# RWKV-7 attention and a SwiGLU feed-forward: the first chunk without its state terms, and a new order of all steps

## The chip, the cores and the metric

The kernel runs on one core of a Trainium2 chip. Such a core has TensorE (PE) for matrix products, with PEld for its weight loads, VectorE (DVE), ScalarE (ACT), GpSimd (POOL) and SyncE (SP); SP, ACT and POOL issue DMAs, and each engine works through its own instructions in order. The engines wait for each other by semaphores. The metric is the device time of one execution in microseconds, the median of several; lower is better.

## The reference

Two blocks follow each other: a recurrent attention over 768 steps for 4 x 8 heads of width 40, and a feed-forward layer on its output (3072 tokens of width 320, inner width 1536).

```python
state = np.zeros((B, H, D, D), dtype=np.float32)
for t in range(S):
    kt, vt, rt = (k[:, :, t], v[:, :, t], r[:, :, t])
    wt, at, bt = (w[:, :, t], a[:, :, t], b[:, :, t])
    y[:, :, t] = np.einsum('bhd,bhde->bhe', rt, state)
    Sa = np.einsum('bhde,bhe->bhd', state, at)
    state_decay = state * wt[:, :, None, :] - np.einsum('bhd,bhe->bhde', Sa, bt)
    state = state_decay + np.einsum('bhd,bhe->bhde', vt, kt)
...
rms = np.sqrt(np.mean(x * x, axis=-1, keepdims=True) + 1e-06)
xn = x / rms * rms_g
g = xn @ w_gate
silu = g * (1.0 / (1.0 + np.exp(-g)))
val = xn @ w_val
return (silu * val @ w_out).astype(np.float32)
```

The state is zero at the start. The weights of the feed-forward layer come as 64-bit numbers, and the kernel turns them into 32-bit ones itself.

## The kernel before

The 768 steps are cut into 24 chunks of 32. Within a chunk the recurrence becomes products and a triangular solve; only the state goes from chunk to chunk. The work of a chunk c has these stages:

- `front(c)`: loads k, v, w, a, b of the chunk (tiles `wan`, `kbn`, `wn`, `VU`), turns them on TensorE, and builds by five levels of doubling (groups `gramk`) the triangular matrix `LT`, the scaled keys `KN` and the decays `T`. At its end `LT` goes out to DRAM and comes back turned as `M`.
- `inverse(c)`: the triangular solve on VectorE: 31 rounds of two small operations (`tmp<-Yi,M` and `Yi<-Yi,tmp`), in sequence. Its result goes out and back into `LT` by DMA.
- `main(c)`: with the state `ST` and its turned copy `Sd`. A group `state` and a first group `lower` make the right side X; a second group `lower` multiplies it by the inverse; `update` gives the new state, to which VectorE adds the old one, decayed (`Sdec`). Then the output, with r loaded for two chunks at a time: `score`, masks (`As`), five `level` groups and a `y0` group (the part that comes from the state), decays and additions of `y` on VectorE, two turns, the norm.
- `feed(g)`: for every two chunks the feed-forward layer on 256 tokens, in twelve slices of the inner width taken in pairs: groups `h64` and `h` (gate and value), the silu on ScalarE (`sg`), a product on VectorE (`hT`), and `out`, which sums over the slices in PSUM (`po`).
- `narrow(f, h, ...)`: once per half slice, the change of weights from 64 to 32 bits: loads into a buffer `wf`, eight steps on VectorE and ScalarE (those on VectorE with one input are TENSOR_SCALARs of 128x480, such as `ex<-wf`; one of three buffers for `ex` is the tile `o`), and a store into `sW` in DRAM.

None of this code issues an instruction when it runs. Each call of `pe`, `tt`, `copy`, `dma`, `blank` and so on makes a `Piece` (L258), and `plan.issue(ORDER, PAIRS)` (L993) issues the pieces in an order that stands in the file as a list of numbers, `ORDER` (L45): each number is the place of the next piece among those not issued yet, and "-" is a filler, a product of the identity with itself into an unused part of `po` (L991). `PAIRS` (L247) says for each use of PSUM which of three double banks (`ps0` to `ps2`) it gets. What matters of the order is each engine's own sequence, and with it what a queue holds up.

The zeros that pad the tiles are set by GpSimd at the start: `blank` is a MEMSET, and `Turns` (L587) calls it for the tiles that ask for it (`wan`, `kbn`, `rn`, `wn`, `VU`, `ST`, `LT`, `Sd`, `A`, `y`; each recorded at L514). They are pieces like all others and have their place in the order. GpSimd also issues most loads of `front` after the first chunk (recorded at L518). All VectorE operations of helpers are recorded at L475, copies of ScalarE at L502, activations at L498, groups of products at L521, turns at L524.

Of the kernel before, what the change touches and what calls it, by code (L numbers as in the profile page):

```python
# [16 lines left out]
P = 128  # L17
# [28 lines left out]
27 33 37 36 26 32 42 38 39 348 40 41 1 110 31 43 0 26 1 14 27 263 - 17 194 2 28 0 41 342 - 16 18 0 41 14 42 43 - 55  # L46
60 72 175 47 84 48 58 186 44 45 8 185 589 54 59 - 70 - - 68 93 69 601 176 49 - 53 - 590 179 16 57 71 80 180 603 50 -
81 92 67 65 624 56 613 51 626 - 66 - 614 52 - 188 64 187 627 178 - 637 - 177 0 8 - - 188 - 60 82 61 78 76 - 81 77
637 75 - 62 388 90 599 624 601 72 194 87 88 74 89 384 73 590 101 196 195 395 84 85 94 197 591 96 86 394 209 385 399
93 592 102 201 202 213 212 225 223 0 94 213 - 10 592 225 223 - 388 - 237 - 233 197 - 395 - - 246 - - 593 - 613 594 -  # L50
- - 221 614 595 234 385 596 615 649 397 - 198 202 - 648 616 617 647 - 207 386 - - 4 328 597 206 602 618 603 210 646
- 220 619 203 218 96 0 603 203 329 16 - 204 208 213 97 0 0 242 33 216 6 34 23 2 0 173 589 590 604 81 201 325 591 199
380 220 219 11 83 163 164 214 313 592 216 326 174 228 200 210 610 213 655 0 299 626 300 359 187 583 584 199 565 287
615 1069 577 197 629 198 211 585 586 362 183 566 587 1068 616 0 78 125 135 302 0 0 87 299 151 302 0 0 0 0 0 300 72
301 311 81 322 837 324 0 0 0 246 844 126 0 126 294 0 0 296 132 302 840 0 0 129 131 0 827 304 0 - 242 130 315 297 327
296 241 0 0 0 0 295 0 295 305 0 296 307 0 316 0 0 543 - 298 0 0 0 0 0 297 310 0 278 0 278 0 - 278 0 290 - - 317 - -
0 0 289 0 283 301 58 261 0 0 - 0 0 301 280 291 246 296 109 281 300 0 0 307 254 105 245 292 0 103 292 305 304 0 0 0
102 286 297 0 0 298 285 312 0 0 - 0 0 0 0 291 0 0 248 0 287 0 293 0 296 801 94 0 0 788 93 789 471 300 0 93 483 94 95
797 96 292 471 472 0 289 483 464 96 97 472 98 99 290 484 100 101 465 466 102 473 515 103 104 105 474 295 294 485 106
107 0 295 292 474 107 108 475 485 476 486 109 110 111 515 492 493 112 487 494 488 113 114 115 116 1 3 0 493 115 0  # L60
378 379 371 0 179 406 0 406 385 0 0 0 - 375 0 382 383 375 0 - - 414 - - - 413 - 383 - - - - - - - - 0 - - - - - - -
- - - - - - - - - - - - - - - - - - - - - - - - - - - - - 0 - - - - - - - - - - 410 - - 409 382 383 - - 0 0 0 370 33
- 35 37 - 36 0 0 0 - 0 0 29 - - - - - 0 40 32 0 0 0 38 - 372 373 411 41 30 39 81 410 - 0 91 231 42 43 51 81 41 373
46 - 48 45 39 229 49 44 90 - 0 46 57 58 0 398 - 52 399 385 386 228 0 0 0 397 634 50 384 637 0 0 0 48 246 0 51 394
150 0 401 631 0 1 2 0 637 398 390 391 376 146 43 377 626 399 638 392 218 378 636 147 635 393 400 430 47 431 148 48
149 49 - 150 50 - 151 401 402 152 242 153 154 - 51 379 243 0 379 642 644 842 - 832 154 155 643 419 833 645 51 380
657 52 646 156 662 674 157 158 - 647 686 649 53 54 402 650 651 843 - 159 656 655 660 55 160 - 161 671 - 56 57 673 -
652 706 162 1 658 163 659 669 2 164 3 0 - 610 608 107 335 603 108 612 609 - 614 109 - - 595 - 110 624 - 625 - 111
636 - - 596 - - - - - - 605 - 112 - 590 345 382 373 - - 782 346 383 607 384 626 622 792 620 113 114 - 115 627 - -
374 375 385 783 - 606 116 635 - 617 - - - 793 - 117 623 376 118 - 619 377 119 378 621 120 618 160 634 121 - 379 122  # L70
- 633 - 380 - - 161 123 124 386 125 381 163 - 164 387 - 388 162 - - 126 127 - 128 629 - - - 389 390 - 631 - 391 129
130 131 630 - 167 639 - 132 133 134 135 640 168 638 - 392 393 430 - 641 136 - 137 138 394 - 165 581 - 431 139 140
141 166 644 - - 142 171 571 721 143 570 580 643 144 145 - 173 - 645 - 175 146 147 148 - 174 172 182 178 - 179 149 -
- 177 637 180 642 150 - 176 189 185 186 432 187 191 732 190 778 788 787 0 282 283 37 18 584 1064 626 1065 284 625
583 41 628 582 568 635 19 498 42 43 285 44 643 286 0 480 637 44 568 598 498 499 500 644 286 501 502 570 45 287 288
503 908 898 643 600 645 494 504 601 657 505 662 506 3 897 649 674 0 649 45 705 46 906 47 - 494 1 506 660 669 659 672
670 48 0 622 633 598 636 645 - 632 458 - 459 0 - 595 0 595 458 853 642 0 360 755 - 765 361 - 505 - 764 362 363 364
500 504 508 507 365 501 502 516 518 503 0 0 45 0 514 43 363 364 365 512 366 367 41 417 419 421 368 369 2 - 3 - - -
370 371 372 418 0 - 372 0 416 426 0 - 369 504 37 426 370 371 372 373 374 375 376 377 378 379 380 381 526 429 525 521
520 505 382 0 482 466 9 396 390 - 377 391 393 392 400 398 343 430 378 387 397 - - 440 344 429 439 580 394 395 408  # L80
345 403 388 11 700 0 0 0 401 402 700 403 343 344 473 345 406 0 406 0 705 708 402 697 474 406 407 707 487 0 0 5 406 0
406 470 485 693 703 8 407 469 480 37 483 0 0 335 41 402 30 480 336 337 338 0 0 400 0 40 39 400 335 336 337 472 0 337
703 705 400 401 699 907 37 338 470 481 402 478 27 704 339 340 479 899 700 341 701 343 486 714 403 28 889 50 719 0
861 673 451 684 677 530 531 313 869 458 11 0 682 867 878 19 554 0 0 9 699 683 684 10 0 10 710 11 12 0 0 38 39 11 551
527 12 0 23 37 659 669 36 704 - 436 670 681 679 539 296 682 680 692 691 703 24 660 677 3 678 676 4 675 435 0 656 657
658 667 432 0 0 40 0 426 19 290 20 685 42 707 292 291 679 21 665 681 41 22 433 40 53 666 30 680 686 23 0 288 681 30
0 30 432 433 434 692 22 674 690 0 0 8 653 0 8 9 667 651 662 0 16 25 17 37 9 0 26 8 400 654 0 652 8 651 38 400 - 39 -
- 37 - - 667 659 - - 469 9 - - - 401 402 403 10 668 16 17 661 0 0 392 650 24 460 461 458 0 36 458 461 8 37 392 647
14 393 15 394 16 395 49 50 47 5 396 397 17 18 19 462 463 729 0 3 583 21 22 458 14 15 392 572 4 461 646 0 0 388 568
640 18 389 11 19 577 390 0 622 0 6 370 371 618 0 435 28 440 0 14 431 438 5 436 370 6 26 432 693 694 7 440 8 0 0 432  # L90
362 0 7 427 686 441 425 0 361 0 440 6 7 430 0 0 352 7 732 353 0 0 0 351 352 13 0 727 8 442 422 352 423 737 353 735
738 726 354 355 356 736 357 419 0 354 355 356 5 730 357 721 358 359 360 361 362 363 364 365 6 0 419 420 742 365 366
367 368 369 423 370 371 372 373 424 0 0 674 423 424 425 6 0 737 732 746 368 369 370 0 429 419 420 735 992 993 1003
1150 668 1002 670 1151 669 685 730 439 368 584 732 421 731 0 0 3 367 368 369 583 370 983 420 584 585 734 586 587 371
735 742 686 421 422 423 424 685 745 756 740 743 992 758 747 744 982 746 757 755 759 768 767 0 3 424 735 0 0 0 0 581
582 772 745 747 583 744 421 730 584 365 746 731 732 431 0 3 440 584 585 586 740 2 425 587 588 1 589 590 741 591 783
365 742 752 366 761 762 757 592 756 368 367 0 5 172 173 174 175 176 337 6 0 333 346 332 176 0 346 176 330 8 9 0 224
176 177 178 179 180 181 9 12 182 183 184 185 186 187 188 561 225 189 190 226 10 227 0 224 0 226 180 181 6 0 0 13 0
214 223 325 178 179 180 181 182 183 184 185 186 187 13 188 189 190 215 224 191 192 193 276 267 0 263 274 414 20 323
222 223 191 192 193 194 334 324 0 4 331 194 330 332 195 226 229 230 225 0 222 223 226 227 240 239 532 232 4 0 229 4  # L100
0 7 12 233 234 333 193 317 326 321 324 533 334 235 239 540 331 332 531 532 236 543 13 14 240 335 241 195 242 243 244
612 8 196 245 541 542 336 548 0 193 5 190 242 0 328 329 330 0 541 330 331 236 543 539 332 237 238 737 239 240 6 745
538 540 544 552 545 735 397 557 569 581 556 16 746 555 542 728 566 551 546 736 241 565 398 727 550 553 563 568 738
# [290 lines left out]
def kernel(  # L394
# [34 lines left out]
    B, H, S, D = r.shape  # L429
# [5 lines left out]
    NCH = S // C  # L435
# [364 lines left out]
    def main(c):  # L800
# [21 lines left out]
        if c + 1 < NCH:  # L822
            tt(ST_.next()[:, :, :, 0:D].rearrange("p n i d -> p i n d"),
               up[:, :, 0:N * D].rearrange("p i (n d) -> p i n d", n=N),
               Sdec.rearrange("p (n i) d -> p i n d", n=N), ADD)
# [198 lines left out]
```

## Time and profile before

Three runs took 1142.61, 1139.24 and 1142.14 us, the median being 1142.14. The profiled execution took 1138.7 us, with a span of 1136.9 us from its first to its last instruction.

| engine | busy us | share of the span | instructions |
|---|---|---|---|
| PE | 1042.0 | 92% | 23166 |
| PEld | 858.4 | 76% | 23166 |
| DVE | 912.9 | 80% | 3069 |
| ACT | 447.8 | 39% | 988 |
| POOL | 303.5 | 27% | 533 |

Of the PE's busy time 66.3 us are the fillers (446 records, two for each). The costliest groups are those of the feed-forward layer, 358.1 us for gate and value and 182.1 us for the last product, and on VectorE the two operations of the solve, 157.9 and 155.9 us. The chain of work that ended last lies on PE for 56% of the span, on DVE for 29%, and 6% of it is time in which an engine waited for nothing that the profile shows ("issue").

The page cuts the span into 40 equal slices and gives each engine's busy share in tenths, and for PE the granted clock, in tenths of full speed. Other views give sums for a stretch of time, the operations of one tile with their durations (least, median, most), or the instructions in order of time. [...]

### The profile page before, as it was taken

What the parts mean: (1) busy time and instruction counts of PE and PEld (TensorE: products, weight loads), DVE (VectorE), ACT (ScalarE), POOL (GpSimd) and SP (SyncE); (2) the same over time, 40 slices, a digit from 0 to 9 for tenths busy, and PEclk for the clock granted to TensorE, in tenths of its full rate; (3) what the DMA queues carried; (4) which work ended last, traced back from release to release, by engine and by line L of the source; (5) the groups of instructions that cost most, each with busy time, mean ns of one, the idle gap of its engine ahead of it and who ended that gap; (6) DMA issues with size and microseconds to landing.
All of it is one profiled execution on the core that took longest, in us unless ns stands there. A gap on an engine that the chain in (4) does not pass through costs nothing.

```text
span 1136.9 us, 53105 instructions
## 1 busy us (share of the span) xinstructions
PE 1042.0 (92%) x23166; PEld 858.4 (76%) x23166; DVE 912.9 (80%) x3069; ACT 447.8 (39%) x988; POOL 303.5 (27%) x533
## 2 busy tenths in 40 slices
PE   5678889889999999999999999999989999999998
PEld 4667778667778777778877877777768787777876
DVE  5899999799787998799699699889878799697421
ACT  4543544653253343344333434334335335323211
POOL 6530333113223223223223313332313423100000
PEclk9769899899999999999999999999999999999999
DMA  7445442776555546446545545545546545444242
GB/s 152 98 106 170 119 119 63 206 224 159 136 138 123 120 102 153 128 109 153 134 117 134 126 116 141 133 116 142 116 100 158 122 111 141 102 112 124 77 151 64
DMA packets 171177, 145.43 MB, mean 128 GB/s; under 512 B 123712, under 2 KB 142080, under 8 KB 170944
## 3 DMA queue, kind: packets, MB, share of 16 engines
q1 hardware_dynamic: 152576, 119.06, 38.9%
q0 software_dynamic: 16192, 22.64, 10.3%
q8 instruction: 182, 2.98, 1.1%
q10 hardware_dynamic: 2176, 0.33, 0.2%
q14 instruction: 51, 0.42, 0.1%
HBM read 125.83 MB, written 16.12 MB: 125 GB/s over the span
## 4 chain that ended last, share of the span: by engine, by line
PE 56%; DVE 29%; issue 6%; DMA 3%; ACT 3%; POOL 2%; SPq 1%; DVEq 0%; ACTq 0%; POOLq 0%
PE ps L521 37%; PE po L521 10%; PE ps L524 7%; DVE Yi L475 5%; DVE tmp L475 5%; DVE LT L475 3%; DVE K L475 3%; DVE y L475 2%; DVE hT L475 1%; DVE Ab L475 1%; POOL kbn L518 1%; DVE ex L475 1%; DVE As L475 1%; PE po L991 1%; DMA wan<-in_w_dram 1%
## 5 line engine op out<-in xcount | busy, mean ns | idle before, releaser
L521 PE MATMUL ps<-xg,wf 128*128 128x256 f32 (+1 forms) x1728 | 358.1, 395 | 7.0 <-DVE hT L475 1.7
L521 PEld LDWEIGHTS ps<-xg,wf 128*128 128x128 f32 (+1 forms) x1728 | 264.7, 191 | 64.1 <-issue 18.4
L521 PE MATMUL po<-wf,hT 128*128 128x320 f32 x576 | 182.1, 448 | 2.9 <-DVE hT L475 2.9
L475 DVE TENSOR_TENSOR tmp<-Yi,M 128x60 f32<-128x60 f32 (+24 forms) x744 | 157.9, 212 | 18.4 <-DMA M<-sB 1.0
L475 DVE TENSOR_TENSOR Yi<-Yi,tmp 128x60 f32<-128x60 f32 (+24 forms) x744 | 155.9, 210 | 17.4
L498 ACT ACTIVATE sg<-ps 128x256 f32<-128x256 f32 x144 | 54.0, 384 | 242.0 <-PE ps L521 231.6
L518 POOL DMA_DIRECT2D VU<-in_v_dram x92 | 53.2, 585 | 351.7 <-PE ps L521 193.7
L521 PEld LDWEIGHTS po<-wf,hT 128*128 128x128 f32 x576 | 103.0, 191 | 38.1 <-DVE hT L475 5.0
L475 DVE TENSOR_TENSOR hT<-ps,sg 128x256 f32<-128x256 f32 x144 | 59.8, 421 | 64.7 <-ACT sg L498 63.5
L521 PEld LDWEIGHTS ps<-Ab,K 40*64 40x64 f32 x4608 | 78.2, 138 | 33.5 <-issue 19.3
L521 PE MATMUL ps<-Ab,K 40*64 40x56 f32 x4608 | 87.8, 225 | 15.7 <-DVE Yi L475 5.7
L502 ACT COPY KN<-ps 128x640 f32<-128x640 f32 x96 | 66.4, 691 | 79.5 <-PE ps L521 37.5
L475 DVE TENSOR_TENSOR K<-K,T 128x512 f32<-128x512 f32 (+1 forms) x192 | 92.6, 490 | 4.5 <-PE ps L521 2.6
L475 DVE TENSOR_TENSOR As<-ps,msi 128x256 f32<-128x256 f32 (+1 forms) x192 | 82.8, 483 | 10.8 <-PE ps L521 10.8
L502 ACT COPY K<-K 128x256 f32<-128x256 f32 (+1 forms) x168 | 71.7, 443 | 46.2 <-DVE K L475 24.1
L521 PEld LDWEIGHTS ps<-As,KN 128*40 128x40 f32 x3072 | 65.4, 123 | 17.9 <-issue 10.8
L518 POOL DMA_DIRECT2D kbn<-in_b_dram x92 | 53.9, 588 | 93.5 <-PE ps L521 91.9
L518 POOL DMA_DIRECT2D wn<-in_w_dram x92 | 51.9, 570 | 99.6 <-DVE tmp L475 47.7
L521 PE MATMUL ps<-As,KN 128*40 128x32 f32 x3072 | 72.8, 204 | 4.0 <-issue 2.6
L518 POOL DMA_DIRECT2D kbn<-in_k_dram x92 | 53.5, 585 | 71.5 <-PE ps L521 62.3
L991 PE MATMUL po<-ident 128*128 128x128 f32 x446 | 66.3, 302 | 5.3 <-ACT po L544 5.3
L475 DVE TENSOR_TENSOR y<-y,ps 128x256 f32<-128x256 f32 x120 | 50.4, 420 | 23.2 <-PE ps L521 18.5
(123 smaller groups left out, 1571.7 us busy)
## 6 DMA issues: line engine op xcount, KB each, us to landing
wf<-sW SPq DMA_DIRECT2D x144, 480.0 KB, 4.1
M<-sB SPq DMA_DIRECT2D x96, 128.0 KB, 3.8
rn<-in_r_dram SPq DMA_DIRECT2D x24, 160.0 KB, 4.4
sW<-ex SPq DMA_DIRECT2D x16, 240.0 KB, 3.7
out_dram<-o SPq DMA_DIRECT2D x48, 80.0 KB, 3.7
kbn<-in_b_dram POOLq DMA_DIRECT2D x92, 40.0 KB, 3.3
wan<-in_w_dram POOLq DMA_DIRECT2D x46, 80.0 KB, 3.8
wan<-in_a_dram POOLq DMA_DIRECT2D x46, 80.0 KB, 4.0
```

The costliest lines, as they stand in the source:

```text
L475: plan.add("DVE", time + more + each * size(o), 0.087, lambda at: fn(at(o), *m(at)), [o], aps(*args))
L498: scalar(o, [a], lambda at: nc.scalar.activation(at(o), at(a), f, **kw), aps(acc), 0.1 if f in (AF.Square, AF.Relu) else 0.0)
L502: scalar(o, [a], lambda at: nc.scalar.copy(at(o), at(a)), extra=more)
L518: plan.add(by, 0.6 if by == "POOL" else 0.45, 0.0, lambda at: queue.dma_start(out=o, in_=i), [o], [i], load=LOADS[load], since=since)
L521: return o, lhsT, rhs, lambda at: nc.tensor.matmul(at(o), lhsT, rhs, start=start, stop=stop, skip_group_check=True), 4
L524: return o, i, ident, lambda at: nc.tensor.transpose(at(o), i, ident), 2
L991: plan.warm = lambda: nc.tensor.matmul(po_[:, 0, DM:DM + P], ident, ident, start=False, stop=False, skip_group_check=True)
```

## The change

Two things change. First, chunk 0 drops the terms of the state, which is zero there: the `state` group, the decay `Sdec`, the addition of the decayed state (the new state is a copy by ScalarE instead), the `y0` group with its copy and its decay, and the addition of level 16, for which half of `y` is set to zero by GpSimd and the other half copied by ScalarE. Second, `ORDER` and `PAIRS` are new from end to end.

```diff
-        pe("state", [mm(X[other(i, n), o, col(n % 4)], ...
-        pe("lower", [mm(X[other(i, n), o, col(n % 4)], LT[own(i, n), o * N + slot(n)], VU[own(i, n), n, o, 0:D], False, n % 4 == 3)
+        if c > 0:
+            pe("state", [mm(X[other(i, n), o, col(n % 4)], ...
+        pe("lower", [mm(X[other(i, n), o, col(n % 4)], LT[own(i, n), o * N + slot(n)], VU[own(i, n), n, o, 0:D], c == 0 and n % 4 == 0, n % 4 == 3)
...
-        tt(Sdec, ST.rearrange("p n i d -> p (n i) d")[:, :, 0:D], z["T"][32].to_broadcast((P, NI, D)), MUL)
+        if c > 0:
+            tt(Sdec, ST.rearrange("p n i d -> p (n i) d")[:, :, 0:D], z["T"][32].to_broadcast((P, NI, D)), MUL)
...
-        if c + 1 < NCH:
+        if c == 0:
+            copy(ST_.next()[:, :, :, 0:D].rearrange("p n i d -> p i n d"), up[:, :, 0:N * D].rearrange("p i (n d) -> p i n d", n=N))
+        elif c + 1 < NCH:
...
-        pe("y0", [mm(y0[part(o), i, n], ...
+        if c > 0:
+            pe("y0", [mm(y0[part(o), i, n], ...
...
-        copy(yi[:, :, :, 0:16], y0[:, :, :, 0:16])
-        tt(yi[:, :, :, 16:], y0[:, :, :, 16:],
-           z["T"][16].rearrange("p (n i) x -> p i n x", i=2)[:, :, :, 0:1].to_broadcast((P, 2, N, 16)), MUL)
-        down(4, yl[:, 0])
+        if c > 0:
+            copy(yi[:, :, :, 0:16], y0[:, :, :, 0:16])
+            tt(yi[:, :, :, 16:], y0[:, :, :, 16:],
+               z["T"][16].rearrange("p (n i) x -> p i n x", i=2)[:, :, :, 0:1].to_broadcast((P, 2, N, 16)), MUL)
+            down(4, yl[:, 0])
+        else:
+            blank(y[:, :, 0:16], 0.0)
+            copy(y[:, :, 16:], yl[:, 0].rearrange("p n (i l) -> p (n i) l", i=2))
```

`ORDER` has 6131 pieces and 223 fillers before, 6127 pieces and 280 fillers after. What the new order does to GpSimd's first instructions, from the two programs' lists (a load is one DMA issue):

```
before  ... load kbn2 | ST0 rn0 y1 wn0 VU0 Sd0 ST1 VU1 | load VU1, load kbn2, 3 loads VU1 | y0 | loads
after   ... load wan | ST0 | load kbn2 | kbn2 y1 | 3 loads kbn2 | rn0 y0 | load kbn2 | wn0 VU0 | load VU1 |
            Sd0 ST1 | load VU1, load kbn2 | y0 (half) | 2 loads VU1 | VU1 | loads
```

The names without "load" are MEMSETs of these tiles; the half `y0` is the new one.

## The prediction

> **What bounds the kernel now.** I read the busy share over time first, then the sums of single stretches, then the timeline of the places these pointed to. In the page's second part the digits are busy tenths in slices of 28.4 us:
>
> ```profile
> PE   5678889889999999999999999999989999999998
> DVE  5899999799787998799699699889878799697421
> PEclk9769899899999999999999999999999999999999
> ```
>
> The kernel has two parts. In the first eight slices (to about 230 us) VectorE is at 8 to 9 and TensorE below it; from the ninth on TensorE is at 9. The sums by stretch say it sharper (columns: stretch, its length, busy us and count of PE, PEld, DVE, ACT, POOL, granted clock, DMA share, GB/s):
>
> ```profile
> 35.00:41.00 6.00, 0.00 (x0) 0.00 (x0) 5.97 (x5) 1.47 (x4) 6.00 (x12) 0.87 0.08 17
> 41.00:82.00 41.00, 30.37 (x776) 27.50 (x776) 37.67 (x120) 22.23 (x46) 9.41 (x16) 0.67 0.48 119
> 98.00:233.00 135.00, 115.78 (x2904) 99.85 (x2908) 121.61 (x390) 66.60 (x138) 37.43 (x62) 0.92 0.50 132
> 233.00:1090.00 857.00, 817.87 (x18825) 665.80 (x18812) 706.33 (x2423) 328.22 (x746) 221.88 (x378) 0.99 0.51 127
> ```
>
> From 41 to 233 us VectorE is busy 90 to 92%, and part of TensorE's time is filler. The same query for the filler products alone (columns: PE and PEld busy, clock, DMA):
>
> ```profile
> 82.00:98.00 16.00, 15.42 (x130) 15.23 (x129) 0.94 0.70 181
> 98.00:233.00 135.00, 31.86 (x214) 27.72 (x214) 0.92 0.50 132
> ```
>
> Without the filler TensorE is busy 84 of these 135 us. So VectorE's queue sets the start, and what is saved on TensorE there is worth nothing. From 233 to 1090 us TensorE works 95% of the time; only its own work and its 39 us of idle count. Behind that comes the last feed-forward group on TensorE alone.
>
> In one place the start does no work: in the timeline from 34 us (start, duration, engine, operation; rows in between left out).
>
> ```profile
> 34.52 0.66 DVE L475 TENSOR_SCALAR wf<-wf 128x480 int32<-128x480 int32 x1
> ...
> 35.11 5.04 DVE L475 TENSOR_SCALAR o<-wf 128x480 int32<-128x480 int32 x1
> ...
> 35.32 0.97 POOL L514 MEMSET ST<- 128x1024 f32 x1
> 36.21 0.44 POOL L514 MEMSET rn<- 128x384 f32 x1
> 36.57 0.54 POOL L514 MEMSET y<- 128x512 f32 x1
> 37.04 0.65 POOL L514 MEMSET wn<- 128x640 f32 x1
> 37.61 0.44 POOL L514 MEMSET VU<- 128x384 f32 x1
> 37.98 0.65 POOL L514 MEMSET Sd<- 128x640 f32 x1
> 38.55 0.97 POOL L514 MEMSET ST<- 128x1024 f32 x1
> 39.44 0.44 POOL L514 MEMSET VU<- 128x384 f32 x1
> 39.81 0.58 POOL L518 DMA_DIRECT2D VU<-in_v_dram  x1
> ```
>
> A TENSOR_SCALAR that takes 0.40 us at the median lasts 5.04: it ends just after GpSimd's eight MEMSETs, which stand in one run. VectorE counts as busy, but 4.64 us of it is a stall, and the chain of waits of the first 120 us runs through this row.
>
> **The change part by part.**
>
> *Work left out of chunk 0.* On VectorE four operations go: the decay of the state, its addition, and at the output the decay and the addition of level 16. Their rows, from the views of these tiles up to 130 us:
>
> ```profile
> L475 DVE TENSOR_TENSOR Sdec<-ST,T x2: 824/834/844, 46.2 to 106.1; 128x640 f32<-128x640 f32 x2
> L475 DVE TENSOR_TENSOR ST<-ps,Sdec x1: 825/825/825, 105.3 to 105.3; 128x640 f32<-128x640 f32 x1
> L475 DVE TENSOR_TENSOR y<-ps,T x2: 417/418/419, 63.9 to 122.9; 128x256 f32<-128x256 f32 x2
> ```
>
> That is 0.84 + 0.82 + 0.42 + 0.42 (a y<-y,ps of 128x256) = 2.5 us, all before 115 us, on the bound engine. TensorE loses two groups of 32 products (`state`, `y0`), 0.8 to 1.2 us each there; filler stands around them, so nothing. ScalarE loses one 128x256 copy (0.36), gains one (0.36) and one of 128x640 (0.69, the mean of KN<-ps of that size); it is busy 22 of 41 us, so nothing. GpSimd gains a MEMSET of 128x256, about 0.35 us by the 128x384 row (0.44).
>
> Is the 2.5 us in front of what decides? In the instruction lists I summed, by the trace's durations, the VectorE work that stands ahead of the last step a product needs, directly or through others. For chunk 3's second `lower`, where TensorE becomes dense (232.6 us), it is 201.6 us before and 199.1 after: **-2.5**. TensorE's work still to come at that point is the same in both orders, 838.9 us, each kind at its median. So nothing that the new order moves ahead of this point or behind it eats the gain.
>
> *GpSimd's queue.* The new order puts the MEMSETs apart: between the first ST and the second there is a DMA issue after every two at most, the longest pair Sd+ST, 0.65+0.97 = 1.62 us. Does that help? **Here a rule and the row differ.** The Trainium skill ("SBUF — State Buffer", Who interferes with whom) says that VectorE in a 2-port mode, which it lists for tensor_scalar, and GpSimd share a port pair, and that whoever comes second is blocked for the whole instruction of the other. By that the row should have lost at most one MEMSET, 0.97 us; spreading the MEMSETs would bring nothing, and the sum below would be -3.0 us; the added MEMSET would even be one more blocker. The row lost eight: it shows no release between MEMSETs whose spans touch, and the release at the DMA issue. The neighbour at 34.52 agrees: it met only DMA issues and took 0.66, 0.26 over. I follow the row. In the new order six such TENSOR_SCALARs stand in the stretch of some 12 us in which 5.7 us of MEMSETs run: six, times a half, times half a mean run (0.57) gives 1.7 us, against 5.0 now (4.64 + 0.26 + 0.14 of one at 42.39). Ends: nothing lost, or all 5.7. **-3.3**.
>
> *What is then late next?* The loads of M in front of the first inverse stand in SP's queue behind a weight load that was issued at 41.66, after VectorE freed its buffer (operations at 40.26 and 40.94); so they move forward with the stall. The new SP queue puts three wn loads (0.6 us each) in front of M; the first inverse began at 58.4 with M's last issue at 48.7, and this slack covers them. The first loads: five kbn loads instead of four stand behind ScalarE's wait for `eye`, 0.46 us more, against a MEMSET of 0.44 for a copy of 0.7 in front of `eye`: nothing.
>
> *Fillers.* 223 become 280, each two records, 0.22 us at full clock, 0.28 at the mean. TensorE's queue is in order, so a filler costs where real work is ready behind it. Of the 57, 28 stand where TensorE now idles for 2.2, 2.0 and 3.0 us (62 to 78 us), and 19 where one `y0` group now takes 5 us (207.4 to 212.5): free. The run before chunk 0's second `lower` goes from 66 to 71; now it ends 0.8 us before that product can start, and the new order puts 1.8 us more VectorE work between its start and the product: free. Nine more behind that product stand before a gap of 1.7: free. Twelve stand between chunk 3's `lower` and the next feed-forward product, 3 now: 9 x 0.22 = 2.0 us, half of it taken up by gaps of 1.7 us some microseconds later. **+1.0**, ends 0 and 16 (57 x 0.28).
>
> *The order of the dense part.* All of it is new, so its 39 us of idle is drawn again. What can be counted: between the work that a product needs from VectorE and the work that VectorE can do before it needs TensorE again lie 5.3 us on average in both orders, below 2 us at 8.4% of TensorE's time before and 7.6% after: no sign either way. Neighbours of different kinds cost more: by the timeline a `level` group takes 0.61 us behind its own kind and 0.74 behind another, `out` 1.08 and 1.27, `h` 1.73 and 1.92. Behind the last filler there are 445 changes of the array's layout between 792 groups before, 434 after: 11 x 0.15 = **-1.6**. Of the k, v and b loads on GpSimd's queue nine in ten have at least 9.0 us of TensorE work between release and use (before 9.5), over their landing times of 3.3 us: nothing.
>
> Sum: -2.5 - 3.3 + 1.0 - 1.6 = **-6.4 us**. The profiled execution took 1138.7 us (span 1136.9), so its counterpart is 1132.3; the shown runs have a median 3.4 above it, so I predict **1135.7** for the median.
>
> **The rivals.**
>
> *The gain at the start is lost (1140.5).* The stall returns elsewhere (six places can meet a run), or the start is bound by transfers: after the first inverse its result travels out and back for 15 us (83 to 98) whatever VectorE does. Then only the changes of layout remain, -1.6. For it: 16 us of filler there. Against it: VectorE has work in that time, 15.0 of 16 us.
>
> *Slower: the dense part waits more (1149).* TensorE now waits 0.65 to 0.7 us before many first feed-forward groups, and nothing in the list of instructions tells how an engine's lateness runs on. One more such wait for each of the 21 chunks from 233 us on costs 21 x 0.65 = 13.7 us, so 1149.4. It decides from 6.4 + 3.4 = 9.8 us more idle on, a quarter more than the 39 us. Against it: the equal slack counted above.
>
> *Fillers in the way (1143.5).* If TensorE runs ahead of the plan that placed them, the 12 and the 16 in front of chunk 5's first gram products are paid in full: 28 x 0.28 = 7.8 us.
>
> **How the numbers follow.** Forecast 0.58, its own range 1130 to 1139; gain lost 0.20; dense part slower 0.14; fillers 0.08. A measurement can tell about 0.3% from no change, 3.4 us. Faster: 0.93 of the forecast and a fifth of the second case, 0.58. No change: 0.06 of the forecast, 0.7 of the second and of the fillers, 0.24. The rest, 0.18, is slower. Range 1129 (no stall left and 5 us less idle) to 1147 (most of the slower case's extra wait).
>
> **What would show it.** No TENSOR_SCALAR over 2 us in the first 50 us; the first inverse's first operation near 54 us, not 58.4; chunk 3's second `lower` near 227; TensorE idle from there to the last group near 39 us. I am wrong if that `lower` comes at 231 or later, or if it is early and the end is not.

## The result and the profile after

The changed kernel takes **1110.83 us** (median of four runs, 1108.33 to 1112.72) against 1142.38 us (four runs, 1139.24 to 1147.14) for the kernel before: ratio **0.9719 [0.9678, 0.9760]**, some 31.5 us less. The forecast said faster, but 1135.7 us, with a range that ended at 1129. The profiled execution took 1109.57 us, with a span of 1107.8 and a mean granted clock of 0.981 (before: 1138.7, 1136.9, 0.972).

The busy tenths in 40 slices of the kernel after, now of 27.7 us each:

```profile
PE   5698889989999999999999999999999999999998
DVE  5999998899798889799789689988878889798421
PEclk9799999989999999999999999999979999999999
```

The sums of its stretches, those of before moved to where its stages now lie (columns as in the prediction):

```profile
41.00:82.00 41.00, 34.34 (x634) 32.34 (x635) 38.37 (x134) 20.09 (x42) 10.70 (x19) 0.83 0.49 109
98.00:216.00 118.00, 104.91 (x2718) 90.63 (x2711) 108.92 (x361) 65.17 (x133) 36.74 (x62) 0.99 0.53 133
216.00:1061.00 845.00, 821.10 (x18871) 670.28 (x18869) 710.52 (x2432) 333.35 (x748) 221.09 (x377) 0.99 0.51 131
```

In the first two rows VectorE is busy 94 and 92% (before 92 and 90): it still sets the start, which is only shorter. The dense part, from chunk 3's second `lower` on, begins at 216.3 us, where it began at 232.6. And it is denser: of the last row's 845 us TensorE is idle 23.9, where it was idle 39.1 of 857 before. The saving has **two halves**. I matched each instruction of both traces with its piece of the program and compared the two times at places with the same TensorE work still to come: at 838.9 us left (chunk 3's second `lower`) the new kernel is 16.2 us ahead, at 600 it is 21.3, at 300 it is 24.3, at the end 29.1. Rather more than half comes in the first 216 us, the rest spread over the stretch behind them.

The timeline in which the long TENSOR_SCALAR of before stood (start, duration, engine, operation), after:

```profile
34.99 2.79 DVE L475 TENSOR_SCALAR ex<-wf 128x480 int32<-128x480 int32 x1
35.11 0.44 POOL L514 MEMSET rn<- 128x384 f32 x1
35.47 0.54 POOL L514 MEMSET y<- 128x512 f32 x1
35.94 0.58 POOL L518 DMA_DIRECT2D kbn<-in_k_dram  x1
36.51 0.65 POOL L514 MEMSET wn<- 128x640 f32 x1
37.08 0.44 POOL L514 MEMSET VU<- 128x384 f32 x1
```

The stall is halved (2.79 us for an operation of 0.40, before 5.04), not gone, and it runs on across the DMA issue at 35.94, which by the prediction's reading should have released it.

To say what the start gained I followed VectorE to the last `tmp` step of the fourth inverse, some 27 us before chunk 3's second `lower`. It is the last step but one (the last one ends at 204.1 us before and at 190.0 after); it is called the end of the fourth inverse below.

| up to there, us | before | after |
|---|---|---|
| end of the `tmp` step | 203.8 | 189.1 |
| VectorE's own time (in a step), from 14.0 us on | 172.4 | 164.6 |
| VectorE idle from there, gaps of any length | 17.4 | 10.5 |
| of it waiting for TensorE | 8.1 | 1.7 |
| steps that stand directly behind their producer in VectorE's queue | 157 | 125 |
| TENSOR_SCALAR time above 0.40 us each | 5.2 | 3.8 |

So 14.7 us: 7.8 of own time and 6.9 of idle, where the forecast knew only own time, 5.8. A further 1.5 us are gained between this step and the `lower`; they were not followed. These are single executions: where e7, e15 and e16 below run the same new start, the step ends at 191.0, 191.8 and 191.1, so a difference of less than some 3 us between two of them says little.

### The profile page after: what moved, and what is told of

Read it like the earlier page. It is cut to its first block, busy times and chain, and to the rows that moved or that the text cites. A ratio compares the mean times of both kernels' runs of the same rounds, so it can differ in the third digit from the quotient of the medians.

```text
span 1107.8 us, 53122 instructions
## 1 busy us (share of the span) xinstructions
PE 1043.1 (94%) x23152; PEld 862.2 (78%) x23152; DVE 906.1 (82%) x3065; ACT 453.9 (41%) x989; POOL 302.4 (27%) x534
## 3 DMA queue, kind: packets, MB, share of 16 engines
q0 software_dynamic: 16192, 22.64, 10.5%
## 4 chain that ended last, share of the span: by engine, by line
PE 59%; DVE 26%; issue 4%; DMA 4%; ACT 4%; POOL 2%; SPq 1%; DVEq 0%; POOLq 0%; ACTq 0%
PE ps L521 40%; PE po L521 11%; PE ps L524 8%; DVE LT L475 4%; DVE tmp L475 3%; DVE Yi L475 3%; DVE K L475 2%; DVE As L475 2%; DVE ex L475 2%; DVE wf L475 2%; DVE y L475 1%; SPq L518 1%; DVE Ab L475 1%; ACT K L502 1%; DVE r L475 1%
## 5 line engine op out<-in xcount | busy, mean ns | idle before, releaser
L521 PE MATMUL po<-wf,hT 128*128 128x320 f32 x576 | 178.6, 444 | 2.7 <-DVE hT L475 1.3
L521 PE MATMUL ps<-Ab,K 40*64 40x56 f32 x4608 | 87.4, 226 | 11.2 <-DVE K L475 3.1
L521 PEld LDWEIGHTS ps<-As,KN 128*40 128x40 f32 x3072 | 67.2, 125 | 18.7 <-issue 10.7
L1000 PE MATMUL po<-ident 128*128 128x128 f32 x560 | 72.9, 284 | 5.3 <-ACT po L544 5.3
L518 POOL DMA_DIRECT2D kbn<-in_b_dram x92 | 53.8, 587 | 83.0 <-PE ps L521 72.3
L1000 PEld LDWEIGHTS po<-ident 128*128 128x128 f32 x560 | 67.6, 197 | 6.7 <-POOL wan L514 5.2
```

The lines of the kernel that those rows point to most:

```text
L518: plan.add(by, 0.6 if by == "POOL" else 0.45, 0.0, lambda at: queue.dma_start(out=o, in_=i), [o], [i], load=LOADS[load], since=since)
L521: return o, lhsT, rhs, lambda at: nc.tensor.matmul(at(o), lhsT, rhs, start=start, stop=stop, skip_group_check=True), 4
L1000: plan.warm = lambda: nc.tensor.matmul(po_[:, 0, DM:DM + P], ident, ident, start=False, stop=False, skip_group_check=True)
```

## Experiments

Four rivals were to be told apart: the terms left out; the MEMSET stall; the clock and the fillers; the order of the queues itself (of VectorE's above all, in the start, in the dense part or in both). Each row's ratio is against the kernel before on the same chip; the rows come from four chips, so two rows are better compared by their ratios than by their medians.

| run | median us (runs) | ratio [95%] | end of the fourth inverse |
|---|---|---|---|
| e1_terms_only | 1140.92 (10) | 0.9988 [0.9959, 1.0018] | 203.6 |
| e2_order_only | 1114.62 (4) | 0.9777 [0.9736, 0.9817] | 199.1 |
| e3_memsets_apart | 1140.78 (10) | 0.9989 [0.9957, 1.0022] | 201.1 |
| e4_memsets_run | 1109.31 (4) | 0.9729 [0.9701, 0.9757] | 191.5 |
| e7_new_start | 1127.12 (5) | 0.9869 [0.9801, 0.9937] | 191.0 |
| e8_old_start | 1130.34 (10) | 0.9908 [0.9873, 0.9944] | 204.5 |
| e5_new_no_fillers | 1160.79 (4) | 1.0155 [1.0084, 1.0226] | 202.1 |
| e9_old_more_fillers | 1146.42 (10) | 1.0034 [1.0000, 1.0069] | 203.8 |
| e11_old_split | 1137.16 (10) | 0.9979 [0.9937, 1.0021] | 200.2 |
| e12_new_split | 1106.53 (4) | 0.9696 [0.9645, 0.9747] | 189.7 |
| e13_old_narrow_up | 1139.94 (10) | 0.9988 [0.9960, 1.0015] | 203.4 |
| e14_old_four_edits | 1131.72 (10) | 0.9935 [0.9904, 0.9966] | 196.6 |
| e15_rest_split | 1119.62 (4) | 0.9812 [0.9752, 0.9871] | 191.8 |
| e16_new_two_thirds | 1116.51 (4) | 0.9785 [0.9739, 0.9831] | 191.1 |

### The two parts of the change, each alone

e1: the code of after, and the order of before without the pieces that no longer exist.

```diff
 code:  as after (chunk 0 without the state's terms)
-ORDER: after's
+ORDER: before's, less the pieces of chunk 0's state, Sdec, ST addition, y0, its copy and decay, level 16
```

> The order of before, piece for piece, with only chunk 0's terms of the state left out (the state's new copy stands where its addition stood, the copy of y where the addition of level 16 stood). Theory A (the terms are 2.5 us of VectorE work in a start that VectorE bounds, and the order brings the rest): 2 to 3 us less than before, ratio 0.998. Theory B (the terms shorten a chain that every later chunk inherits): 8 us less or more, ratio 0.993 or lower. If neither, no change at all: the 2.5 us go into a wait.

e2: the code of before, and the order of after, with the dropped pieces put back beside their neighbours.

```diff
-code:  as after
+code:  as before (all terms of chunk 0)
 ORDER: after's, plus these pieces
```

> The new order with chunk 0's terms put back in (nothing is left out of the computation). Theory A: about 28 us less than before, ratio 0.975, since the order is what counts. Theory B: 20 us less at most, ratio 0.983 or higher.

The terms alone bring 1.3 us, which can't be told from none; VectorE's own time to the fourth inverse falls by 1.5 us (172.4 to 170.9), but 1.3 of it comes back as idle (17.4 to 18.7). The order alone brings 27.6 us, most of it. The put-back pieces cost 3.8 us with the new order by the medians and 6.6 by the ratios (the ranges of the two kernels' runs overlap), and part of it is waits that their places make: one of VectorE on ScalarE's copy of `y0`, near 109 us, takes 2.5 us. In its profiled execution, the longest of the four (1119.03 us), the fourth inverse ends at 199.1 us, only 4.7 us earlier than before and 10.0 later than after: in the new order the put-back pieces cost the start more than their own time. So the **new order** is the subject, and the terms are a small part when they go alone.

### The MEMSETs

e3: the order of before with DMA issues moved in among GpSimd's MEMSETs, at most two of these together.

```diff
-... | ST0 rn0 y1 wn0 VU0 Sd0 ST1 VU1 | load VU1, load kbn2, 3 loads VU1
+... | ST0 | load | rn0 | load | y1 wn0 | load | VU0 Sd0 | load | ST1 | load | VU1 | 2 loads
```

> Before, with one thing changed: the eight MEMSETs that stand in one run on GpSimd have DMA issues between them, two at most together. Theory A (the stall of the TENSOR_SCALAR is a loss of its own size): no TENSOR_SCALAR over 2 us, 3 to 4.6 us less than before, ratio 0.996 to 0.997. Theory C (the stall also lets TensorE's clock fall and delays the loads behind it, so that it costs more than itself): 6 to 12 us less, ratio 0.990 to 0.995, and fewer half-clock windows before 90 us. Against both: the time is the same, and the start waits for something else.

e4: after's order with those MEMSETs gathered in one run again.

```diff
-... ST0 | load | y1 | loads | rn0 | load | wn0 VU0 | load | Sd0 ST1 | ...
+... 3 loads kbn2 | ST0 rn0 y1 wn0 VU0 Sd0 ST1 VU1 | load kbn2 | ...
```

> The changed kernel, with its MEMSETs gathered into a run of eight again. Theory A: a TENSOR_SCALAR of 4 to 5 us in the timeline and 3 to 4.6 us more than the changed kernel, 1114 to 1116. Theory C: 6 to 12 us more, 1117 to 1123.

In e3 the fourth inverse ends 2.7 us earlier, but the total gives only 1.4 us, within its interval. Its timeline shows three shorter stalls in place of one of 5.04 (together 3.7 us over 0.40 each, so that e3 does not show what a start without the stall would gain):

```profile
34.56 0.97 POOL L542 MEMSET ST<- 128x1024 f32 x1
34.95 2.25 DVE L503 TENSOR_SCALAR wf<-wf 128x480 int32<-128x480 int32 x1
35.45 0.58 POOL L546 DMA_DIRECT2D kbn<-in_b_dram  x1
36.02 0.44 POOL L542 MEMSET rn<- 128x384 f32 x1
36.38 0.58 POOL L546 DMA_DIRECT2D kbn<-in_k_dram  x1
37.12 1.37 DVE L503 TENSOR_SCALAR o<-wf 128x480 int32<-128x480 int32 x1
...
40.73 1.24 DVE L503 TENSOR_SCALAR wf<-wf 128x480 int32<-128x480 int32 x1
```

The first of them is held through the whole issues at 35.45 and 36.38. e4 costs nothing (1109.31, after 1110.83): with the same run of MEMSETs, after's VectorE queue reaches it later and has but one TENSOR_SCALAR there.

```profile
33.68 0.97 POOL L544 MEMSET ST<- 128x1024 f32 x1
...
35.89 2.61 DVE L505 TENSOR_SCALAR ex<-wf 128x480 int32<-128x480 int32 x1
...
37.80 0.44 POOL L544 MEMSET VU<- 128x384 f32 x1
```

It meets only the second half of the run, and ends 0.26 us after the run's last MEMSET. Its fourth inverse ends at 191.5 us, between the 189.1 to 191.8 of the other runs with the new start. So the spread of the MEMSETs, half of the forecast's gain, explains at most 2 to 3 of the 31 us; in the new order it explains none that was seen.

### Start or dense part

e7 has the new order up to some 258 us and the old one behind; e8 the old one up to some 265 us and the new one behind. Both leave out chunk 0's terms.

```diff
-ORDER: before's (terms out)
+ORDER: e7: after's pieces up to 258 us, then all others in before's order
+ORDER: e8: before's pieces up to 265 us, then all others in after's order
```

> Chunk 0's terms left out. The new order up to about 258 us (1480 pieces), then all remaining pieces in the order of before. Theory D (two gains of their own, 16 us up to chunk 3's second lower and 13 us in the dense part): 12 to 17 us less than before, ratio 0.985 to 0.990. Theory E (all of it is the start, the dense part only inherits): 25 us less, ratio 0.978 or lower. Theory F (all of it is the dense order; the early start is given back): ratio 0.997 or higher.

> Chunk 0's terms left out. The order of before up to about 265 us, then all remaining pieces in the new order. Theory D: 12 to 15 us less than before, ratio 0.987 to 0.990, so that this and the new start add up to the whole. Theory E: ratio 0.997 or higher. Theory F: ratio 0.978 or lower.

By the ratios the new start alone brings 1.3%, 15.0 us of 1143.33, and the new dense part alone 0.9%, 10.5 us. The product of the two ratios is 0.978; the whole gives 0.972. **Two gains that add up**, as the comparison of the two traces said. e16 cuts the dense part in turn: after's order to about 690 us, before's behind.

```diff
-ORDER: e7: after's pieces up to 258 us, then all others in before's order
+ORDER: after's pieces up to 690 us, then all others in before's order
```

> Chunk 0's terms left out. The new order up to about 690 us, the old one from there. If the gain in the dense part accrues evenly (theory N): two thirds of the way from the new start with the old rest (1127) to the new order (1110), 1114 to 1119. If it sits in the last 130 us, where the two traces part by another 3 to 5 us (theory O): 1120 or more.

1116.5 lies between e7's 1127.1 and after's 1110.8, 0.65 of the way (0.56 by the ratios), with half of the stretch from 258 us to the end in the new order: the gain lies on both sides of 690 us, not at one place.

### The clock and the fillers

The time in which TensorE ran at half clock before 230 us falls from 51.2 to 20.5 us. Was that the start's gain? e9 puts into before's order as many fillers in front of each group as the new order has; e5 takes all fillers out of the new order.

```diff
-ORDER: before's, 223 fillers
+ORDER: e9: before's, 280 fillers, after's number in front of each group
-ORDER: after's, 280 fillers
+ORDER: e5: after's without any
```

> Before, its own order, with nothing changed but the fillers: as many in front of each group of products as in the new order (280 in all). Theory G: 6 to 12 us less than before, ratio 0.990 to 0.995, fewer half-clock windows between 60 and 85 us. Theory H: the same as before within 0.3%, or slower where fillers stand in the way.

> The changed kernel without any of its 280 fillers (they compute nothing that is used). Theory G (the new start gains because its fillers keep TensorE's clock up: 20 us at half clock before chunk 3's second lower, against 51 before the change): many half-clock windows again and 8 to 16 us more than the changed kernel, 1118 to 1126. Theory H (the order of the real work does it): within 4 us of the changed kernel, or faster.

The clock of e9, page, part 2:

```profile
PEclk9799899998999999999999999999999899999999
```

That is the new kernel's clock (half clock before 230 us: 23.9 us) on the old order, and the fourth inverse ends at 203.8 us as before; the total is no better, 1.0034. So the faster clock alone isn't the start's gain. The same line of e5:

```profile
PEclk9755579889989999999999899999989999999999
```

Without fillers the start runs at 0.75 of the clock (116.1 us at half clock before 230 us), and a further 57.7 us fall to half clock behind it (after: 22.8). The fourth inverse ends 13.0 us later than after's, the kernel 50 us later: the fillers are worth more than the whole change. But the clock is only a part of it. The additional 34.9 us at half clock behind 230 us cost at most half of that, 17 us, and 25 us, partly in the same stretches, are waits of TensorE for its own instructions (34.0 us in e5, 8.7 in after; they are shown under "Neighbours in the dense part").

### Neighbours in VectorE's queue

In all traces a VectorE step that stands directly behind the step that makes its input begins 0.034 us after that one's end (5 to 95%: 0.034 to 0.035). An independent step begins 0.083 us before its neighbour's end (median). Each dependent neighbour thus costs 0.117 us. The solve is made of them; the VectorE timeline of before:

```profile
58.58 0.19 DVE L475 TENSOR_TENSOR Yi<-Yi,tmp 128x31 f32<-128x31 f32 x1
58.81 0.19 DVE L475 TENSOR_TENSOR tmp<-Yi,M 128x30 f32<-128x30 f32 x1
59.04 0.19 DVE L475 TENSOR_TENSOR Yi<-Yi,tmp 128x30 f32<-128x30 f32 x1
```

A step every 0.23 us, each of 0.19. After, the same stage of the same chunk:

```profile
55.81 0.18 DVE L475 TENSOR_TENSOR tmp<-Yi,M 128x28 f32<-128x28 f32 x1
55.93 0.45 DVE L475 TENSOR_TENSOR Ab<-A,T 128x192 f32<-128x192 f32 x1
56.30 0.18 DVE L475 TENSOR_TENSOR Yi<-Yi,tmp 128x28 f32<-128x28 f32 x1
56.40 0.42 DVE L475 TENSOR_TENSOR T<-T 128x256 f32<-128x256 f32 x1
```

Other work stands between the solve's steps, and each row begins before the one above it has ended. Up to the fourth inverse the new order has 32 dependent neighbours fewer, 3.7 us; behind it 39 fewer of 1082. The price is a median's: some independent steps begin 0.034 us after their neighbour's end too, 14 in the start of before and 22 in that of after, so that of all such late beginnings there are 24 fewer, 2.8 us.

e11 does this alone on the order of before, in the start: where b follows its producer a, and the next step c needs neither, c goes between them. 23 swaps, 157 to 127 neighbours.

```diff
-VectorE: ... a  b(needs a)  c ...
+VectorE: ... a  c  b ...
```

> Before, with 23 swaps of neighbours in VectorE's queue up to the end of the fourth inverse, so that 127 steps instead of 157 stand directly behind the step whose result they read (the new order has 125); nothing else is moved or left out. In the traces a step behind its own producer starts 0.034 us after that one's end, any other 0.083 before it. Theory J (each such neighbour costs 0.117 us where VectorE bounds): that end 3.5 us earlier, and the whole 2 to 4 us shorter, ratio 0.997. Rival: the swaps delay steps that others wait for, no gain, ratio 0.999 to 1.003.

The fourth inverse ends 3.6 us earlier (203.8 to 200.2): the price per neighbour holds. The total of 0.9979 can't be told from none.

### The rest of the start

What VectorE waited for up to the fourth inverse (us in total, times, longest), the longest waits for products in the list of its waits, before:

```profile
DVE LT L475 <- PE ps L521: 4.2, 4, 1.8
DVE y L475 <- PE ps L521: 1.9, 3, 1.4
DVE K L475 <- PE ps L521: 1.4, 1, 1.4
```

and after:

```profile
DVE K L475 <- PE ps L521: 1.0, 1, 1.0
DVE LT L475 <- PE ps L521: 0.7, 1, 0.7
```

Two of these stand close together at 26 to 31 us before, with one for ScalarE between them. With the waits (idle before it <- releaser) in brackets, VectorE's timeline of before:

```profile
26.98 0.69 DVE L475 TENSOR_TENSOR K<-K,T 128x512 f32<-128x512 f32 x1 [1.42 <-PE ps L521]
28.00 0.43 DVE L475 COPY_PREDICATED LT<-msk,ps 128x256 f32<-128x256 uint32 x1 [0.33 <-ACT KN L502]
...
30.57 0.44 DVE L475 COPY_PREDICATED LT<-msk,ps 128x256 f32<-128x256 uint32 x1 [1.83 <-PE ps L521]
```

and after:

```profile
26.85 0.69 DVE L475 TENSOR_TENSOR K<-K,T 128x512 f32<-128x512 f32 x1
27.60 0.66 DVE L475 SCALAR_TENSOR_TENSOR ex<-wf,ex 128x480 int32<-128x480 int32 x1
28.29 0.41 DVE L475 TENSOR_SCALAR wf<-wf 128x480 int32<-128x480 int32 x1
28.62 0.42 DVE L475 COPY_PREDICATED LT<-msk,ps 128x256 f32<-128x256 uint32 x1
```

The waits of 3.6 us in brackets are gone from these steps, and two more steps of `narrow` stand among them. e13 moves the first `narrow`'s steps (three of VectorE, two of ScalarE) up into these waits in before's order.

```diff
-front(0): K  LT  K  Ab  K  aP  [wait] K  [wait] LT  narrow1  [wait] LT
+front(0): LT  narrow1  K  Ab  K  aP  K  narrow2  narrow3  LT  [wait] LT
```

> Before, with five steps of the first weight conversion (three of VectorE, two of ScalarE) moved up into the two places near 26 and 29 us where VectorE waits 1.4 and 1.8 us for TensorE; nothing is left out. Theory K (VectorE's waits for TensorE in the start, 8.1 us before and 1.7 after the change, are a matter of what stands in its queue then): these waits fall by 2 to 3 us and so does the whole, ratio 0.9975. Rival (the clock or TensorE's own lateness decides): the waits move a few steps on, ratio 0.999 or higher.

A **miss**. The waits become 1.5 us shorter, but the last one keeps 1.59 of its 1.83 us (`LT` at 30.09), and the fourth inverse ends 0.4 us earlier: what TensorE does for that step comes no sooner, and later work of VectorE has less to fill its own waits. e14 joins the four edits: terms out, MEMSETs apart, swaps (158 to 130) and `narrow` moved up.

```diff
 ORDER: before's
+terms of chunk 0 out (e1), MEMSETs apart (e3), swaps in the start (e11), narrow's steps up (e13)
```

> The order of before with four edits together: chunk 0's terms left out, the MEMSETs apart, the neighbours split, the weight conversion moved up. If the start is the sum of these (theories A, J, K): the end of the fourth inverse 8 to 11 us earlier, and the whole 8 to 10 us shorter, ratio 0.991 to 0.993; the new start alone, with chunk 0's terms left out, gave 0.987. Rival: they overlap, 5 us or less, ratio 0.996 or higher.

1131.72 us, 7.2 us earlier at the fourth inverse and 7.4 by the ratio at the end, somewhat less than expected: half of the start's gain is thus built by hand. The other half is mostly waits for TensorE (8.1 us before, 6.1 here, 1.7 after) that no single edit of mine removed; a part of them is explained below, with TensorE's instruction blocks.

### Neighbours in the dense part

If the dense part's gain were VectorE's shorter time, more swaps there would bring much. e15 takes e7 and makes 151 swaps in its old-order rest (1083 to 886 dependent neighbours); e12 takes the changed kernel and makes 148 over its whole length (1168 to 967, 20 of them in the start).

```diff
 ORDER: e7's        (e15: behind 258 us)
 ORDER: after's     (e12: everywhere)
-VectorE: ... a  b(needs a)  c ...
+VectorE: ... a  c  b ...
```

> Chunk 0's terms left out. The new start with the old rest, as run before (1127), with 151 swaps of neighbours in VectorE's queue in the rest alone: 197 fewer steps directly behind their producer, 23 us of VectorE's time. Theory L (the dense part is shorter in the new order because VectorE has fewer such neighbours there, 1043 against 1082, and so is late less often): five times that difference should more than make up the 13 us, 1112 to 1120. Theory M (TensorE's own sequence and what it waits for, not VectorE's spare time): 1123 to 1128.

> The changed kernel, with 148 swaps of neighbours in VectorE's queue over its whole length: 967 steps instead of 1168 directly behind their producer, 104 instead of 124 of them in the start. Theory J: 2 us less from the start; in the dense part VectorE gets 21 us of free time, which counts only where TensorE waits for it, 0 to 6 us: in all 1103 to 1108 against about 1110. Rival (the dense part hangs on single late steps, which the swaps delay): 1110 to 1116.

197 neighbours fewer in e15, 23 us of VectorE by the price above, bring 7.5 us against e7 by the medians and 6.5 by the ratios (the ranges of the runs just overlap). At that rate, a third, the 39 fewer of the new order are worth 1.5 us of the dense part's 10 to 13. So this is **not the dense part's main cause**. e12 has the lowest median of all, 1106.53 us, but it can't be told from the changed kernel: the ratios differ by 0.0023 (2.6 us) and their intervals overlap. By its page VectorE is busy 892.9 us, 13.2 less than after's 906.1, with the same instructions (201 neighbours at the 0.083 us that overlap would be 16.7; the gap of 0.034 never counted as busy); TensorE is busy 1043.3 us, after's 1043.1.

What else differs in the dense part shows in the groups of TensorE's products, from chunk 3's second `lower` on (line, engine, operation, count; busy, mean ns; idle before them and what ended it). Before:

```profile
L521 PE MATMUL ps<-xg,wf 64*128 64x256 f32 (+1 forms) x1512 | 312.2, 393 | 6.4 <-DVE hT L475 1.7 <-ACT Ab L502 1.4 <-issue 1.2
L521 PE MATMUL ps<-rE,vut 40*64 40x32 f32 x1344 | 24.7, 220 | 5.0 <-issue 2.7 <-ACT vut L502 1.7 <-DVE LT L475 0.4
L524 PE MATMUL ps<-ident,K 128*128 128x128 f32 x144 | 19.5, 277 | 3.5 <-ACT Ab L502 1.4 <-ACT Xs L505 0.7 <-ACT T L502 0.6
L521 PE MATMUL ps<-ST,aP 40*32 40x40 f32 x1280 | 16.3, 201 | 2.7 <-issue 1.0 <-ACT Sd L502 0.8 <-ACT KN L502 0.8
```

and after:

```profile
L521 PE MATMUL ps<-xg,wf 64*128 64x256 f32 (+1 forms) x1512 | 314.2, 395 | 1.3 <-DVE xg L475 0.9
L521 PE MATMUL ps<-rE,vut 40*64 40x32 f32 x1344 | 25.0, 223 | 1.8 <-ACT vut L502 1.1 <-issue 0.6
L524 PE MATMUL ps<-ident,K 128*128 128x128 f32 x144 | 19.1, 275 | 0.1
L521 PE MATMUL ps<-ST,aP 40*32 40x40 f32 x1280 | 15.9, 201 | 0.5 <-ACT A L502 0.5
```

The four rows idle 17.6 us before and 3.7 after, most of it behind copies of ScalarE and "issue"; the other groups together 21.8 and 19.9, some more and some less than before. Over all, from that `lower` to the last product, TensorE's idle fell from 39.8 to 24.5 us, while its busy time did not fall (859.8 and 862.2; without fillers 859.0 and 859.4). By what ended the idle (gaps over 0.1 us) it is "issue" 15.1 us before and 6.6 after, VectorE 14.3 and 10.8, ScalarE 9.1 and 6.1.

The largest fall is in "issue", time in which the profile shows nothing that TensorE waits for. But these waits have fixed places. I counted TensorE's instructions, with a weight load for each product and the semaphore instructions. Of the 264 such waits of over 0.3 us behind 20 us in all sixteen traces, 253 stand at one place of a count by 256 (number 192 or 193 behind a multiple of 256). And the page of before lists a DMA queue of kind "instruction" (packets, MB, share):

```profile
q8 instruction: 182, 2.98, 1.1%
```

These are 182 packets of 16.4 KB, and TensorE's 46635 instructions make 182 blocks of 256. Behind nearly every one of the waits TensorE goes on 1.2 to 1.65 us after the packet of that number has landed. So TensorE waits there, at the beginning of a block, for **its own instructions**. Two of these waits stand in the start of before, each in the middle of a group of products that VectorE needs:

```profile
26.22 0.67 PE L521 MATMUL ps<-Ab,K 40*64 40x56 f32 x27 [0.98 <-issue]
...
111.61 0.38 PE L521 MATMUL ps<-As,KN 128*40 128x32 f32 x10 [1.43 <-issue]
112.03 0.42 DVE L475 TENSOR_TENSOR y<-y,ps 128x256 f32<-128x256 f32 x1 [1.37 <-PE ps L521]
```

Behind the first stands the wait of 1.42 us at 26.98 that is shown above. So some 2.3 us of the 6.4 by which VectorE's waits for TensorE fell are such block ends; after has neither of the two. In all they come to 6.7 us in the start and 13.7 in the dense part before, and to 2.1 and 6.6 after: as TensorE's time is counted, 7.1 of the 12.8 us that the dense part gained. All nine runs with the old dense part have 11.2 to 14.6 us there; after, e2, e4 and e12 have 5.7 to 7.2, e16 6.8. But it is not the order of the work alone that decides: e8 (from 265 us on) and e5 have the new order there too, and 10.6 and 30.7 us; both have fewer fillers, which moves the block ends. No run moved the block ends alone. Why some blocks come late and most don't, and which moves shortened the other waits, stays **open**.

## Why the prediction was right in sign and wrong in size

- *Work left out of chunk 0, -2.5.* Mis-sized, and small. e1 has 1.5 us less of VectorE's own time at the fourth inverse, but ends there only 0.2 us earlier, since 1.3 us come back as idle. In the new order the same terms come to 3.8 us (e2 against after, ranges overlapping), their waits among it; at the fourth inverse they come to 10.0 us in the one execution that was profiled.
- *The stall, -3.3.* Mis-sized. TENSOR_SCALARs above 0.40 us each cost 5.2 us before and 3.8 after: -1.4. "No TENSOR_SCALAR over 2 us" failed at 2.79. Its reading, "the release at the DMA issue", held in the row it came from and fails in after and in e3, where the operation waits through whole issues. The rule of the Trainium skill ("SBUF — State Buffer", Who interferes with whom), read as the prediction read it, one MEMSET at most, fails more plainly: e4's operation waits for five. (The prediction's sum by that rule would be -3.1, not -3.0.) The first inverse did begin "near 54" (53.8), but not for the reason given: at its row the stall became 2.25 us shorter, not 5, and the waits at 26 to 31 us, which the forecast had not looked at, were gone.
- *The sum up to chunk 3's second `lower`.* **The step that failed first.** "So nothing that the new order moves ahead of this point or behind it eats the gain" compared work, at mean durations. The work is indeed equal, but the stage's end was set by more than work: a step takes 0.117 us longer where it stands behind its producer (0.083 of it own time, 0.034 idle; 3.7 us less up to here), and VectorE idled 17.4 us there, which the sum took as unchanged and the new order cut to 10.5. Forecast 227, measured 216.3.
- *The dense part.* **The step that failed second.** "its 39 us of idle is drawn again" and "no sign either way", with equal slack counted on average. The slack's average was the wrong measure: the waits stand at single places, behind late steps of VectorE and ScalarE (23.4 us before, 16.9 after) and at the ends of TensorE's instruction blocks (13.7 and 6.6), and the average of 5.3 us says nothing of these. The part gave 10 (e8) to 13 us (comparison of the two traces). The groups' idle with its releasers was at hand: no proof of a gain, but room for one as large as the loss that a rival was given, and the range allowed only 5 us of it. Nothing in the forecast looked for late blocks: that they became fewer, and so a part of the gain whose sign it had right, is luck.
- *Layout changes, -1.6.* Not isolated; TensorE's busy time without fillers did not fall in the dense part (859.0 and 859.4 us).
- *Fillers, +1.0.* Not shown either way. 57 more on the old order come to 3.9 us (e9, interval from none to 7.9), but at the new order's places without fillers the kernel is 50 us slower (e5). That they bring the clock of the start to full was not foreseen; on the old order it gained nothing (e9). One reading failed: the `y0` group that "now takes 5 us" holds a wait of 3.7 us at a block end (to 211.61), which moves with the number of fillers.
- *Loads and SP's queue, 0.* Nothing contradicts it: in the list of VectorE's waits up to the fourth inverse there is none for a DMA after (one of 0.4 us, for `wf`, follows at once; before it was 0.8).
- *The rivals.* "Gain lost" (1140.5) describes e1 and e3 well, whose mechanisms were the forecast's; it fails for the order. "Dense part waits more" named the right place with the wrong sign. "Fillers in the way" fails.

So what the forecast counted, terms and MEMSETs, gives 1.3 and 1.4 us when done alone, neither to be told from none, and what it took as neutral gave most: order alone 27.6 of 31.5 us.

## What to carry to other kernels

Where a new order is judged, equal work doesn't mean equal time: count in the engine's list how many steps stand directly behind their producer, and how much of its idle time has work that could stand in it, before putting the idle time down as unchanged. An idle time with no visible cause is worth a count of the engine's instructions: here it stood at the block ends. A stall or a wait that is removed alone in a fixed order comes back for the most part as another wait (e1, e3, e13: 0.2 to 2.7 us at the stage's end, nothing sure at the kernel's), while the same edits together gave 7.4 us. And where another engine is the dense one, a saving still counts in part: of 23 us less on VectorE about a third came through (e15, ranges just overlapping).

## What the runs showed of the hardware that was not expected

- A VectorE step begins 0.034 us after its producer's end when it stands directly behind it, and 0.083 us before its neighbour's end (median) when it is independent. 23 swaps moved the fourth inverse by 3.6 us (e11).
- TensorE can wait for its own instructions, at the beginning of a block of 256: 253 of 264 waits of over 0.3 us without another cause stand there in the sixteen traces. They cost 20.4 us of before, 8.7 of after and 34.0 of e5. What makes a block late is open.
- A TENSOR_SCALAR of 128x480 that meets GpSimd's MEMSETs ends about 0.26 us after the last one of a run (eight in before, five in e4, in after four with a DMA issue among them). A DMA issue of GpSimd behind a MEMSET releases it in some cases (39.81 before, 38.16 in e4) and not in others (35.94 after; 35.45, 36.38 and 41.15 in e3). What decides it is open; spans on that engine are rough.
- Fillers act far beyond their place: 280 of them, 72.9 us of TensorE's busy time, bring the half-clock time before 230 us from 116.1 to 20.5 us, and the kernel 50 us, of which the clock is a part and the waits at block ends 25 us.
